# Attention and gated feed-forward on one core: a new order of evictions, statistics and turnings in the first six rows of the QKV stage

## The chip, the cores and the metric

The kernel runs on one core of a Trainium2 chip. The metric is the device time of one execution in microseconds, less being better. The engines are named as the profile names them: PE is TensorE's matmul stream and PEld its weight loads, DVE is VectorE, ACT is ScalarE, POOL is GpSimd, SP is SyncE, whose queue (SPq) issues nearly all DMAs here.

## What is computed

One layer norm feeds two branches whose results are added to the input: a sliding dilated attention (32 heads of 18, eight keys each at distances 0, 2, ... 14) with its output projection, and a gated feed-forward of width 4608. x is 2048 x 576 in bf16.

```python
def _A_ref(x, wqkv, wo):
    B, S, D = x.shape
    H = 32; Dh = D // H
    W, dil = 8, 2
    qkv = (lambda x, *d: x.transpose(*d))((x @ wqkv).reshape(B, S, 3, H, Dh), 2, 0, 3, 1, 4)
...
    logits = jnp.einsum("bhsd,bhswd->bhsw", q, kg) * scale
    logits = jnp.where(mask[None, None, :, :], logits, -1e9)
    attn = _softmax(logits, axis=-1)
    o = jnp.einsum("bhsw,bhswd->bhsd", attn, vg)
    return (lambda x, *d: x.transpose(*d))(o, 0, 2, 1, 3).reshape(B, S, D) @ wo

def _B_ref(x, w_gate, w_up, w_down):
    g = _silu(x @ w_gate)
    u = x @ w_up
    return (g * u) @ w_down

x = A_x
xn = _layernorm(x, axis=-1)
return x + _A_ref(xn, A_wqkv, A_wo) + _B_ref(xn, B_w_gate, B_w_up, B_w_down)
```

## The kernel before

The 2048 tokens are cut into 16 rows of 128. Token p*16+r lies on partition p of row r, so a row is one [128, 576] tile. The program has two stages.

**The QKV stage** goes through the rows 0 to 15. Row r needs its x, normalized and turned (channels on partitions), as xnT. A row is normalized in this order: two `bn_stats` over its halves (`ln_half`, VectorE, line 214), a `bn_aggr` that makes mean and variance of them (line 216), a square root on ScalarE (`ln_sqrt`, line 226), and `normalize`: a reciprocal (line 231), the subtraction and multiplication over 576 columns (`ln_apply`, line 237) and a copy of 64 columns that pads the row (line 243), all on VectorE. Rows 1 to 4 are turned on TensorE against an identity; for rows 2, 3 and 4 this is `transp_halves` (line 280), ten small matmuls into two PSUM tiles, of which ScalarE copies one and VectorE the other to xnT (line 284). Row 0 and the rows from 5 on are turned by a DMA on SP's queue (`transp_dma`, line 288), issued when the row is normalized. (Row 0's DMA turning is for the feed-forward; its QKV product uses a turning on TensorE and weights its sums by 1/std in the eviction.)

`p_row` issues the 36 matmuls of a row: 18 pairs, each on the two halves of TensorE's rows at once, into four PSUM tiles t[0] to t[3] of 432 columns. The first ten pairs are one half of the sums, the last eight the other half. Between the last eight, at the place `at`, `p_row` calls `between`, and there the next row's turning is issued: `at=(0, 3)` is behind four of the eight pairs, the default `(0, 1)` behind two of them. `p_evac` copies the four PSUM tiles out in six parts: part 0 is t[0] (Q), parts 1 and 2 are t[2] (K and V), parts 3 and 4 are t[1] (Q and K), part 5 is t[3] (V). The parts listed in `dve` go to VectorE (line 366, in row 0 line 368), the others to ScalarE (line 366, in row 0 line 370).

The order of all instructions on each engine is the order of the Python calls, written out by hand: the file switches the scheduler off. So an instruction that waits holds up all that stands behind it on its engine. Each DMA that SP issues takes the next of eight completion semaphores in turn, and its issue waits until the DMA eight places before it has landed.

**The feed-forward stage** goes over four token tiles (tt) of 512 tokens and nine chunks (ch) of 512 columns of the gate and up projections: `g_pair` (line 602) issues 36 pairs of matmuls for a chunk from the slot of `gu` that holds its weights, `load_gu` fills the other slot. Chunk `it` = tt*9+ch is computed while the weights of `it`+1 land; those of `it`+2 are loaded when `it` is done. The down projection (`d_half`, line 631) follows for each token tile. Its weights `wd` come in nine chunks by `load_wd` (line 193). The tile `wd` also holds the loaded and the normalized rows of x in the QKV stage, which is why chunks 0 to 6 come during the first token tile; chunk 7 (columns 16128 to 18431 of the flattened tile) and chunk 8 lie past those rows, which end at column 14335. In the first token tile SP issues, behind chunk `it`=0: the weights of `it`=2, two pieces of `wo`, three stores of V to DRAM and `load_wd(7)`; behind `it`=1: the weights of `it`=3, `load_wd(0)` and three pieces of `wo`. The attention runs on VectorE between the feed-forward's products (`chain`).

Of the kernel before, what the change touches and what calls it, by code (L numbers as in the profile page):

```python
# [70 lines left out]
def kernel(  # L71
# [11 lines left out]
    nc = tc.nc  # L83
# [95 lines left out]
    def load_gu(it):  # L179
        ch, slot = it % NCH, it % NSLOT  # L180
        fc = slice(ch * FC * P, (ch + 1) * FC * P)
        nc.sync.dma_start(gu[:, slot, 0:4, :], B_w_gate[0:512, fc].rearrange("(kt kp) n -> kp kt n", kp=P))  # L182
        nc.sync.dma_start(gu[:, slot, 4:8, :], B_w_up[0:512, fc].rearrange("(kt kp) n -> kp kt n", kp=P))
        nc.sync.dma_start(gu[0:64, slot, 8, :], B_w_gate[512:576, fc])
        nc.sync.dma_start(gu[64:128, slot, 8, :], B_w_up[512:576, fc])
# [6 lines left out]
    def load_wd(ch):  # L192
        nc.sync.dma_start(wd[:, ch * FC:(ch + 1) * FC, :],
                          B_w_down[ch * FC * P:(ch + 1) * FC * P, :].rearrange("(f p) j -> p f j", p=P))

    def new_ps(name):
        return ps.tile([P, 512], f32, name=name, tag="ps")


    ln = {}  # L200
# [6 lines left out]
    sums = {}  # L207

    def ln_half(r, k):
        c, j = divmod(r, 4)  # L210
        xc, xn, mv, rstd = ln[c]
        if k == 0:
            sums[r] = lns.tile([P, 2, 6], f32, name="stats")
        nc.vector.bn_stats(sums[r][:, k, :], xc[:, j, k * HALF:(k + 1) * HALF])  # L214
        if k == 1:
            nc.vector.bn_aggr(mv[:, j, :], sums[r][:].rearrange("p c s -> p (c s)"))  # L216

    def ln_stats(r, n=1):
        for i in range(r, r + n):
            ln_half(i, 0)  # L220
            ln_half(i, 1)

    def ln_sqrt(r, n=1):
        c, j = divmod(r, 4)
        xc, xn, mv, rstd = ln[c]
        nc.scalar.activation(rstd[:, j:j + n], mv[:, j:j + n, 1], ACT.Sqrt, bias=eps_t[:], scale=1.0)  # L226

    def ln_recip(r, n=1):
        c, j = divmod(r, 4)
        rstd = ln[c][3]  # L230
        nc.vector.reciprocal(rstd[:, j:j + n], rstd[:, j:j + n])
# [54 lines left out]
    def transp_dma(r):  # L286
        c, j = divmod(r, 4)
        nc.sync.dma_start_transpose(xnT[:, :, r * P:(r + 1) * P], ln[c][1][:, j, :] if r else xn0)
# [7 lines left out]
    def p_mm(t, g, kt, half, r, start, stop):  # L296
        rows = slice(0, P) if half is None else slice(64 * half, 64 * half + 64)
        return nc.tensor.matmul(t[g][:, 0:G], xT_of(r)[rows, kt, :], w_at(g, kt, rows),  # L298
                                start=start, stop=stop)

    def p_row0_k(t, kt, gs=range(NG)):
        for g in gs:
            p_mm(t, g, kt, None, 0, kt == 0, False)
# [6 lines left out]
    def fence_after(mm):  # L310
        f = nc.gpsimd.engine_nop()
        tc.add_manual_dep(f.ins, mm.ins.name, SYNC, reason="first half done")
        return f

    def fence_before(mm, f):
        tc.add_manual_dep(mm.ins, f.ins.name, SYNC, reason="banks change row tiles")

    def p_row(r, between=None, at=(0, 1), early=(), then=None):


        t = [None] * NG
        fence = {}

        def pair(swap, i, kt):
            for half in range(2):
                g = i + 2 * (half ^ swap)
                if t[g] is None:
                    t[g] = new_ps("qkv_ps")
                mm = p_mm(t, g, kt, half, r, swap == 0 and kt == 0, swap == 1 and kt == 3)
                if swap == 0 and kt == 3 and half == 1:  # L330
                    fence[i] = fence_after(mm)
                if swap and kt == 0 and half == 0:
                    fence_before(mm, fence[i])

        for i, kt in early:
            pair(0, i, kt)
        if then is not None:
            then()
        for swap in range(2):
            for i in range(2):  # L340
                for kt in (0, 1, 2, 3) if swap else (0, 4, 1, 2, 3):
                    if swap or (i, kt) not in early:
                        pair(swap, i, kt)
                    if swap and (i, kt) == at and between is not None:
                        between()
        return t

    def p_evac(r, t, only=range(6), between=None, last=6, dve=(5,)):


        c, j = divmod(r, 4)
        ks, vs = stage[2 * c % 4], stage[(2 * c + 1) % 4]
        vdst = vs[:, j, :].rearrange("p (d h) -> p d h", h=H)
        parts = [
            (QO[:, r, 0:G], t[0][:, 0:G]),
            (ks[:, j, HALF:D], t[2][:, 0:HALF]),
            (vdst[:, :, 0:8], t[2][:, HALF:G].rearrange("p (h d) -> p d h", d=DH)),
            (QO[:, r, G:D], t[1][:, 0:D - G]),
            (ks[:, j, 0:HALF], t[1][:, D - G:G]),
            (vdst[:, :, 8:H], t[3][:, 0:G].rearrange("p (h d) -> p d h", d=DH)),  # L360
        ]
        for n in only:
            if n == last:
                between()
            if r:
                (nc.vector.tensor_copy if n in dve else nc.scalar.copy)(*parts[n])  # L366
            elif n in dve:
                nc.vector.tensor_scalar(*parts[n], ln[0][3][:, 0:1], None, op0=ALU.mult)
            else:
                nc.scalar.mul(*parts[n], ln[0][3][:, 0:1])  # L370
# [24 lines left out]
    dve = Filler()  # L395
# [74 lines left out]
    def normalize(r, n=1):  # L470
        ln_recip(r, n)
        for i in range(r, r + n):
            ln_apply(i)
            if i > 4:
                transp_dma(i)

    def turn(r):
        return lambda: transp_halves(r)
# [21 lines left out]
    t = [new_ps("qkv_ps") for g in range(NG)]  # L500
# [14 lines left out]
    def finish_row0():  # L515
        p_row0_k(t, 3)
        p_row0_rest(t)
        p_evac(0, t, (5, 0, 3, 1, 4, 2), dve=(5, 1, 2))
        ln_half(3, 0)
        load_gu(0)  # L520
        transp_dma(0)

    u = p_row(1, turn(2), (0, 3), ((0, 0), (0, 1), (0, 2), (1, 0)), finish_row0)
    p_evac(1, u, (0, 1, 2, 3, 4), dve=(1, 2))
    ln_half(3, 1)
    ln_open(1)
    ln_half(4, 0)
    ln_sqrt(3)
    p_evac(1, u, (5,), dve=())
    normalize(3)  # L530
    for ring in (Kr, Vr):
        nc.sync.dma_start(ring[0:1, 0:HALO, :], wz[0:1, :].unsqueeze(1).to_broadcast([1, HALO, D]))

    t = p_row(2, turn(3), (0, 3))
    ln_half(4, 1)
    ln_sqrt(4)
    normalize(4)
    ln_stats(5)
    p_evac(2, t, dve=())
    ln_sqrt(5)  # L540
    normalize(5)

    t = p_row(3, turn(4))
    ln_stats(6)
# [9 lines left out]
    for r in range(4, R):  # L554
        t = p_row(r)
# [92 lines left out]
    for tt in range(NTT):  # L648
        for ch in range(NCH):
            it = tt * NCH + ch  # L650
            for p in range(2):
                g_pair(tt, ch, p)
                for j in (2 * p, 2 * p + 1):
                    g_evac(ch, j)
                    if it % NCH < NCH - 1 or p == 0:
                        dve.pump(1.4)
            if ch == NCH - 1:
                dve.drain(lambda: chains[0] > tt)
                for r in range(RT * tt, RT * tt + RT):
                    nc.sync.dma_start_transpose(oT[:, :, r * P:(r + 1) * P], QOP[:, r, :])  # L660
            if it + NSLOT < NTT * NCH:
                load_gu(it + NSLOT)
            if tt == 0:
                if 1 <= ch <= 7:
                    load_wd(ch - 1)
                if ch == 5:
                    load_wd(8)
                for _ in range(3 if ch in (1, 2) else 2):
                    if wo_order:
                        load_wo(wo_order.pop(0))  # L670
                if ch == 0:
                    store(2, 3, 3)
                    load_wd(7)
            if ch == 7:
                for i in (0, 2):
                    nc.sync.dma_start(xr[:, i:i + 2, :], x_v[:, RT * tt + i:RT * tt + i + 2, :])
            if ch == 1 and tt < NTT - 1:
                chain(tt + 1)
        for sub in range(0, RT, 2):
            t, fence = {}, {}  # L680
            for swap in range(2):
                for i in (sub, sub + 1):
                    d_half(tt, i, swap, t, fence)
                    if swap:
                        dve.pump(12.5 if i == sub else 4.0)
                        d_out(RT * tt + i, i, t[i])
# [30 lines left out]
```

## Time and profile before

| | |
|---|---|
| median of 3 runs | 505.66 us (504.88 to 505.94) |
| profiled execution, own time | 505.31 us |
| its span (first to last instruction) | 503.5 us |
| mean granted TensorE clock | 1.00 |
| QKV stage, first feed-forward matmul at | 60.98 us |

The profile is of one execution. A timeline row gives the start and the length in microseconds, engine, line, operation, what is written and read, and how many instructions are merged into the row; in brackets stands how long the engine was idle before it and who ended that. Lengths of neighbouring instructions on DVE and ACT overlap by some hundredths of a microsecond, so the next one may start a little before the last one ends. The chain of waits gives, in order of time, the pieces of the path that ended last.

### The profile page before, as it was taken

Reading aid. Unit: us, or ns where it says so; the run is one execution under the profiler, and the core shown is the slowest. Engines: PE = TensorE matmul, PEld = TensorE weight load, DVE = VectorE, ACT = ScalarE, POOL = GpSimd, SP = SyncE. Lnnn points to the kernel's source line nnn. Section 1 sums busy time; section 2 is a strip of 40 time slices with the busy share of each in tenths; the row PEclk is TensorE's granted clock in tenths of the full one; section 3 lists DMA queues with packets and bytes.
Section 4 is the critical chain, followed back from the end, with each engine's and each line's share of the span. In section 5 each row is a group of like instructions: output and inputs, shape, how many; then the busy total and the mean of one; then the engine's idle time right before and its main releaser. Section 6 shows DMA issues by size and latency. Waiting matters only on the chain.

```text
span 503.5 us, 13277 instructions
## 1 busy us (share of the span) xinstructions
PE 498.8 (99%) x5799; PEld 375.5 (75%) x5799; DVE 329.7 (65%) x480; ACT 200.2 (40%) x415; POOL 2.6 (1%) x9
## 2 busy tenths in 40 slices
PE   9999999999999999999999999999999999999997
PEld 4566654444788888888888888888888888888886
DVE  5788499898998698999898129995990222221001
ACT  4666656655400164555300354558000454553000
POOL 2000000000000000000000000000000000000000
PEclk9999999999999999999999999999999999999999
DMA  8699999879931036446731054455600335452100
GB/s 320 159 196 239 287 295 292 255 246 303 241 107 61 25 107 223 158 127 211 156 98 39 26 187 125 159 183 154 143 25 14 99 108 184 140 191 38 28 14 25
DMA packets 77186, 75.42 MB, mean 150 GB/s; under 512 B 22708, under 2 KB 72528, under 8 KB 77128
## 3 DMA queue, kind: packets, MB, share of 16 engines
q1 hardware_dynamic: 76840, 73.98, 49.8%
q8 instruction: 45, 0.74, 0.6%
q10 hardware_dynamic: 288, 0.59, 0.4%
q14 instruction: 13, 0.11, 0.1%
HBM read 58.76 MB, written 5.90 MB: 128 GB/s over the span
## 4 chain that ended last, share of the span: by engine, by line
PE 97%; DMA 2%; DVE 1%; ACT 0%; issue 0%; SPq 0%
PE g_ps L602 54%; PE d_ps L631 32%; PE qkv_ps L298 10%; DMA gu<-in_B_w_up_dram 2%; PE warm_ps L174 1%; DVE stats L214 0%; PE pt L259 0%; ACT QO L366 0%; ACT rstd L226 0%; DVE xnT L284 0%; ACT hT L366 0%; DVE wd L237 0%; DVE mv L216 0%; ACT ot L645 0%; SPq L182 0%
## 5 line engine op out<-in xcount | busy, mean ns | idle before, releaser
L602 PE MATMUL g_ps<-xnT,gu 64*128 64x512 bf16 x2592 | 281.4, 376 | 0.2 <-DMA gu<-in_B_w_up_dram 0.2
L602 PEld LDWEIGHTS <-gu 64*128 64x128 bf16 x2592 | 206.3, 94 | 73.9 <-DMA gu<-in_B_w_up_dram 0.7
L631 PE MATMUL d_ps<-wd,hT 64*128 64x288 bf16 x2304 | 150.5, 283 | 0.0
L613 ACT ACTIVATE sg<-g_ps 128x512 bf16<-128x512 f32 x144 | 87.4, 607 | 157.1 <-PE g_ps L602 157.1
L631 PEld LDWEIGHTS <-hT 64*128 64x128 bf16 x2304 | 122.6, 94 | 21.7
L615 DVE TENSOR_TENSOR hT<-sg,uc 128x512 bf16<-128x512 bf16 x144 | 60.1, 419 | 94.2 <-ACT uc L614 94.0
L614 ACT CAST uc<-g_ps 128x512 bf16<-128x512 f32 x144 | 85.5, 594 | 0.0
L417 DVE TENSOR_REDUCE PP<-PP 128x64 f32<-128x1152 bf16 x64 | 84.9, 1346 | 0.4
L298 PE MATMUL qkv_ps<-hT,xnT 64*128 64x432 bf16 x540 | 50.5, 343 | 0.8 <-ACT QO L366 0.8
L412 DVE TENSOR_TENSOR PP<-QO,Kr 128x2304 bf16<-128x2304 bf16 (+1 forms) x35 | 43.5, 1250 | 7.6 <-DMA Kr<-hT 7.4
L643 DVE TENSOR_TENSOR ot<-d_ps,xr 128x288 bf16<-128x288 f32 x30 | 12.3, 451 | 51.0 <-PE d_ps L631 51.0
L298 PEld LDWEIGHTS <-xnT 64*128 64x128 bf16 x540 | 29.7, 94 | 20.0 <-ACT QO L366 1.2
L444 DVE TENSOR_TENSOR PP<-Vr,A 128x2304 bf16<-128x2304 bf16 (+1 forms) x35 | 43.3, 1251 | 0.4
L449 DVE TENSOR_TENSOR PP<-PP 128x2304 bf16<-128x2304 bf16 x24 | 32.5, 1354 | 0.3
L631 PE MATMUL d_ps<-wo,xnT 64*128 64x288 bf16 x288 | 27.0, 283 | 0.0
L613 ACT ACT_TABLE_LOAD x5 | 6.4, 1283 | 47.5 <-PE g_ps L602 47.5
L366 ACT CAST hT<-qkv_ps 128x288 bf16<-128x288 f32 (+2 forms) x58 | 21.2, 426 | 0.1
L631 PEld LDWEIGHTS <-xnT 64*128 64x128 bf16 x288 | 17.5, 94 | 2.8
L437 ACT ACTIVATE PP<-PP 128x1024 f32<-128x1024 f32 x4 | 4.2, 1056 | 31.2 <-DVE PP L433 31.2
L645 ACT CAST ot<-d_ps 128x288 bf16<-128x288 f32 x1 | 0.4, 398 | 38.7 <-PE d_ps L631 38.7
L366 ACT CAST QO<-qkv_ps 128x432 bf16<-128x432 f32 (+1 forms) x30 | 12.2, 409 | 8.0 <-PE qkv_ps L298 8.0
L214 DVE BATCH_NORM_STATS2 stats<-wd 128x6 f32<-128x288 bf16 x32 | 12.9, 441 | 2.4 <-DMA wd<-in_A_x_dram 2.4
(53 smaller groups left out, 91.7 us busy)
## 6 DMA issues: line engine op xcount, KB each, us to landing
gu<-in_B_w_gate_dram SPq DMA_DIRECT2D x36, 512.0 KB, 3.8
gu<-in_B_w_up_dram SPq DMA_DIRECT2D x36, 512.0 KB, 5.1
wd<-in_B_w_down_dram SPq DMA_DIRECT2D x9, 576.0 KB, 6.0
kv_d<-hT SPq DMA_DIRECT2D x5, 576.0 KB, 6.1
gu<-in_B_w_gate_dram SPq DMA_DIRECT2D x36, 64.0 KB, 4.8
gu<-in_B_w_up_dram SPq DMA_DIRECT2D x36, 64.0 KB, 4.4
xr<-in_A_x_dram SPq DMA_DIRECT2D x8, 288.0 KB, 4.6
out_dram<-ot SPq DMA_DIRECT2D x16, 144.0 KB, 1.8
```

The costliest lines, as they stand in the source:

```text
L214: nc.vector.bn_stats(sums[r][:, k, :], xc[:, j, k * HALF:(k + 1) * HALF])
L298: return nc.tensor.matmul(t[g][:, 0:G], xT_of(r)[rows, kt, :], w_at(g, kt, rows), start=start, stop=stop)
L366: (nc.vector.tensor_copy if n in dve else nc.scalar.copy)(*parts[n])
L412: nc.vector.tensor_tensor(prod[:, a:b], QO[:, RT * tt + a:RT * tt + b, :], Kr[:, s:s + b - a, :], op=ALU.mult)
L417: nc.vector.tensor_reduce(L[:, w, rs], prod[:, rs].rearrange("p r (h d) -> p r h d", d=DH), axis=AX.X, op=ALU.add)
L444: nc.vector.tensor_tensor(dst[:, a:b], Vr[:, s:s + b - a, :].rearrange("p r (d h) -> p r d h", h=H), A[:, w, a:b].unsqueeze(2).to_broadcas ...
L449: nc.vector.tensor_tensor(dst, acc, pv, op=ALU.add)
L602: mm = nc.tensor.matmul(ring_ps[j][b][:], gu[rows, slot, k, fc], xnT[rows, kt, tok], start=(swap == 0 and kt == 0), stop=(swap == 1 and kt ...
L613: nc.scalar.activation(sg[:], t[0][:], ACT.Silu)
L614: nc.scalar.copy(uc[:], t[1][:])
L615: nc.vector.tensor_tensor(hT[:, ch * FC + j, :], sg[:], uc[:], op=ALU.mult)
L631: mm = nc.tensor.matmul(t[sub][h][:, 0:HALF], a[rows], w[rows, h * HALF:(h + 1) * HALF], start=(swap == 0 and n == 0), stop=(swap == 1 and ...
```

## The change

In rows 0 to 5 the order of VectorE's and ScalarE's instructions is new. Row 0's part 1 goes from VectorE to ScalarE, behind part 4; both halves of row 3's statistics come before row 2's turning is copied, and their `bn_aggr` behind it, ahead of row 1's evictions; row 2's turning is issued one pair of matmuls earlier and row 3's two pairs earlier; the root of row 3 comes between parts 0 and 3 of row 1's evictions on ScalarE; row 4's statistics come behind row 3's normalization, row 5's ahead of row 2's evictions; rows 4 and 5 share one root and one reciprocal. And `load_wd(7)` is issued behind row 1, ahead of row 5's turning on SP's queue, no longer behind chunk 0 of the feed-forward.

```diff
@@ -212,13 +212,16 @@
         if k == 0:
             sums[r] = lns.tile([P, 2, 6], f32, name="stats")
         nc.vector.bn_stats(sums[r][:, k, :], xc[:, j, k * HALF:(k + 1) * HALF])
-        if k == 1:
-            nc.vector.bn_aggr(mv[:, j, :], sums[r][:].rearrange("p c s -> p (c s)"))
+
+    def ln_aggr(r):
+        c, j = divmod(r, 4)
+        nc.vector.bn_aggr(ln[c][2][:, j, :], sums[r][:].rearrange("p c s -> p (c s)"))
 
     def ln_stats(r, n=1):
         for i in range(r, r + n):
             ln_half(i, 0)
             ln_half(i, 1)
+            ln_aggr(i)
@@ -515,30 +518,30 @@
     def finish_row0():
         p_row0_k(t, 3)
         p_row0_rest(t)
-        p_evac(0, t, (5, 0, 3, 1, 4, 2), dve=(5, 1, 2))
+        p_evac(0, t, (5, 0, 3, 2, 4, 1), dve=(5, 2))
         ln_half(3, 0)
+        ln_half(3, 1)
         load_gu(0)
         transp_dma(0)
 
-    u = p_row(1, turn(2), (0, 3), ((0, 0), (0, 1), (0, 2), (1, 0)), finish_row0)
-    p_evac(1, u, (0, 1, 2, 3, 4), dve=(1, 2))
-    ln_half(3, 1)
+    u = p_row(1, turn(2), (0, 2), ((0, 0), (0, 1), (0, 2), (1, 0)), finish_row0)
+    ln_aggr(3)
+    p_evac(1, u, (0, 1, 2), dve=(1, 2))
+    ln_sqrt(3)
+    p_evac(1, u, (3, 4, 5), dve=())
+    normalize(3)
     ln_open(1)
-    ln_half(4, 0)
-    ln_sqrt(3)
-    p_evac(1, u, (5,), dve=())
-    normalize(3)
+    ln_stats(4)
     for ring in (Kr, Vr):
         nc.sync.dma_start(ring[0:1, 0:HALO, :], wz[0:1, :].unsqueeze(1).to_broadcast([1, HALO, D]))
-
-    t = p_row(2, turn(3), (0, 3))
-    ln_half(4, 1)
-    ln_sqrt(4)
-    normalize(4)
+    load_wd(7)
+
+    t = p_row(2, turn(3))
     ln_stats(5)
-    p_evac(2, t, dve=())
-    ln_sqrt(5)
-    normalize(5)
+    p_evac(2, t, (0, 1, 2), dve=())
+    ln_sqrt(4, 2)
+    p_evac(2, t, (3, 4, 5), dve=())
+    normalize(4, 2)
@@ -670,7 +673,6 @@
                 if ch == 0:
                     store(2, 3, 3)
-                    load_wd(7)
```

## The prediction

> **What bounds the kernel now.** I read the page's chain of waits first, then the same chain in order of time, then the timeline of PE and of VectorE around the places where the chain leaves PE.
>
> ```profile
> PE 97%; DMA 2%; DVE 1%; ACT 0%; issue 0%; SPq 0%
> ```
>
> ```profile
> 16.35 0.49 DVE xnT L284
> ...
> 21.38 39.60 PE qkv_ps L298 x432
> ...
> 76.97 7.62 DMA gu<-in_B_w_up_dram
> ...
> 84.64 46.94 PE g_ps L602 x431
> 131.59 39.66 PE d_ps L631 x646
> 171.24 70.04 PE g_ps L602 x648
> ```
>
> PE sets the time but for two places: from row 3's copy at 16.35 to 21.38 the path runs over VectorE and ScalarE, and before 84.64 over the landing of the up weights of chunk 3. Only time that PE loses there can be won. How much it is:
>
> ```profile
> 12.41 0.31 PE L280 MATMUL pt<-ident,wd 64*128 64x64 bf16 x10
> 12.55 3.60 PE L298 MATMUL qkv_ps<-hT,xnT 64*128 64x432 bf16 x36
> 15.98 0.33 PE L280 MATMUL pt<-ident,wd 64*128 64x64 bf16 x10
> 16.12 3.24 PE L298 MATMUL qkv_ps<-hT,xnT 64*128 64x432 bf16 x32
> 19.18 0.33 PE L280 MATMUL pt<-ident,wd 64*128 64x64 bf16 x10
> 19.32 1.28 PE L298 MATMUL qkv_ps<-hT,xnT 64*128 64x432 bf16 x12
> ```
>
> From row 4 on 432 matmuls take 39.60 us without a break, 0.183 for a pair, 3.30 for a row's 36. The 36 between the turnings of rows 2 and 3 take 15.98 - 12.55 = 3.43, so 0.13 is lost; the next 32 take 19.18 - 16.12 = 3.06 in place of 2.93, another 0.13. The last 12 should end at 19.32 + 1.10 = 20.42, and row 4 begins at 21.38: 0.96 lost. That makes **1.22 us in the QKV stage**. In the feed-forward the first token tile lasts from 21.38 + 39.60 = 60.98 to 131.59, 70.61 us, the second 70.04: **0.57 us** more, and the chain has one place in it that is not PE, the weights before 84.64.
>
> The three losses in the QKV stage have one form. Each row waits for the second half of its turning, which VectorE copies:
>
> ```profile
> 10.82 1.37 DVE L368 TENSOR_SCALAR hT<-qkv_ps,rstd 128x432 bf16<-128x432 f32 x3 [0.25 <-PE qkv_ps L298]
> 12.10 0.45 DVE L214 BATCH_NORM_STATS2 stats<-wd 128x6 f32<-128x288 bf16 x1
> 12.79 0.49 DVE L284 CAST xnT<-pt 128x320 bf16<-128x320 f32 x1 [0.23 <-PE pt L280]
> 13.19 0.66 DVE L366 CAST hT<-qkv_ps 128x288 bf16<-128x288 f32 x2
> ...
> 18.57 0.81 DVE L214 BATCH_NORM_STATS2 stats<-wd 128x6 f32<-128x288 bf16 x2
> 19.42 0.21 DVE L216 BATCH_NORM_AGGREGATE mv<-stats 128x2 f32<-128x12 f32 x1
> 19.99 0.16 DVE L231 RECIPROCAL rstd<-rstd 128x1 f32<-128x1 f32 x1 [0.36 <-ACT rstd L226]
> 20.19 0.43 DVE L237 TENSOR_SCALAR wd<-wd,mv,rstd 128x576 bf16<-128x576 bf16 x1
> 20.66 0.18 DVE L243 COPY wd<-wd 128x64 bf16<-128x64 bf16 x1
> 20.75 0.48 DVE L284 CAST xnT<-pt 128x320 bf16<-128x320 f32 x1
> ```
>
> Row 4's copy ends at 21.23 and PE starts at 21.38, 0.15 later; I use 0.15 for every row. (The chain goes over a QO eviction that ends at nearly the same time; the copy fits rows 2 and 3 as well.) PE had turned row 4 at 19.18, but the copy stands on VectorE behind row 5's normalization, which waits for row 5's root on ScalarE (the bracket at 19.99).
>
> **The change part by part.** I follow the new order with these lengths. A VectorE copy of a turning starts 0.38 behind PE's turning (12.79 - 12.41), and the next instruction 0.40 behind its start (13.19 - 12.79). ScalarE:
>
> ```profile
> 12.75 0.42 ACT L284 CAST xnT<-pt 128x320 bf16<-128x320 f32 x1 [0.87 <-PE pt L280]
> 13.07 0.71 ACT L366 CAST QO<-qkv_ps 128x432 bf16<-128x432 f32 x2
> ```
>
> *Row 0's part 1 goes to ScalarE.*
>
> ```profile
> L368 DVE TENSOR_SCALAR hT<-qkv_ps,rstd 128x288 bf16<-128x288 f32 x1 | 0.5, 508 | 0.0
> ```
>
> The instruction itself takes 0.51, 0.43 without its overlap. VectorE is done with row 0 at 12.19 - 0.43 = 11.76 and starts row 3's statistics near 11.68; both halves take 0.81 and end at 12.49. On ScalarE part 1 now waits for VectorE's part 2, as both read t[2]; a wait that was not there. It starts near 11.80 and takes some 0.5 (0.508 above). Behind it stands the copy of row 2's turning, due at 12.23 + 0.34 = 12.57, so the wait has 0.27 of cover; without that cover row 2 would start later by what is missing.
>
> *Row 2's turning one pair earlier*: 12.41 - 0.18 = 12.23. VectorE's copy runs from 12.61 to 13.10, so PE may start row 2 at 13.25. PE wants it after the turning (0.14) and five pairs (0.92), at 13.29. The first 0.13 is gone, by a hair: 0.04.
>
> *Row 3.* `bn_aggr` at 13.01 ends at 13.22; a reciprocal can follow 0.36 later (19.42 + 0.21 to 19.99), root included, so at 13.58 and, as ScalarE's copy at 12.57 and part 0 at 12.89 stand ahead of the root, near 13.65. VectorE meanwhile evicts parts 1 and 2 until 13.72 (13.14 and 0.66, less an overlap of 0.08), then reciprocal, normalization from 13.92, pad until 14.57. The turning stands two pairs earlier, behind 12 pairs (2.20) of a row that starts at 13.29: 15.49. It has 0.9 to spare. Row 4's statistics run from 14.48 to 15.53, ahead of the copy, which starts at 15.87 and ends at 16.36; PE may start row 3 at 16.51 and wants it at 15.49 + 0.14 + 1.10 = 16.73. The second 0.13 is gone, with 0.22 to spare.
>
> *Rows 4 and 5 together.* Row 5's statistics follow the copy, 16.27 to 17.33 (0.81, 0.04, 0.21). The joint reciprocal follows 0.36 later, at 17.69, since ScalarE is through parts 0 to 2 of row 2 by then (their 576 + 144 columns from 16.2 on, some 0.9 by the 0.71 of two such parts above); row 4's normalization begins 0.20 later, at 17.89, and its pad ends at 18.54; row 5's take from 18.45 to 19.10. PE turns row 4 behind 12 pairs of row 3: 16.73 + 2.20 = 18.93, 0.4 after its pad. VectorE is free at 19.01, so the copy goes from 19.31 to 19.79, PE may start row 4 at 19.94 and wants it at 18.93 + 1.24 = 20.17. So PE meets no wait, and **row 4 starts at 20.17 in place of 21.38: 1.21 us won**. From there VectorE is 1.44 ahead of its old times (20.75 to 19.31) and PE 1.21, so rows 5 to 15, which had no wait, get none. The bounds of this part: 1.22 is all that was lost; if each of the some ten links between 15.87 and 19.31 were 0.1 longer than in the rows, row 4 would start 0.7 late and 0.5 would be won.
>
> *The load of chunk 7.* It is 576 KB on a queue that is in use:
>
> ```profile
> 5.00:18.00 13.00, 12.98 (x136) 7.03 (x136) 9.82 (x32) 6.43 (x20) 1.73 (x3) 1.00 1.05 356
> 18.00:22.00 4.00, 3.22 (x46) 1.85 (x43) 3.45 (x12) 3.25 (x12) 0.00 (x0) 1.00 0.01 3
> 60.00:69.00 9.00, 9.00 (x89) 4.75 (x84) 8.90 (x8) 6.33 (x14) 0.00 (x0) 1.00 0.98 313
> 69.00:76.50 7.50, 7.50 (x72) 3.96 (x70) 7.50 (x10) 3.84 (x8) 0.00 (x0) 1.00 0.81 262
> 76.50:92.40 15.90, 15.74 (x144) 7.45 (x141) 12.29 (x22) 11.43 (x19) 0.00 (x0) 1.00 1.01 304
> ```
>
> The last two columns are the DMA engines' busy share and GB/s. In the old place the chunk (0.59 MB) goes out just ahead of chunk 3's weights into a full stretch: at 304 GB/s it holds what is behind it for 1.9 us. Those weights are 0.57 late. Whether the queue keeps its order or the transfers share it, 0.59 MB less has to pass before they have landed; a third of the 1.9 is enough. So **0.57 won**; if the next chunk becomes the late one, part of it comes back, so the bounds are 0 and 0.57. In the new place it stands behind two small issues, of which this is the last:
>
> ```profile
> 13.93 0.82 SPq L532 DMA_DIRECT2D Vr<-ot  x1
> ```
>
> So it is issued near 14.8, when the weights of chunk 0 still fill the queue, and needs 0.59 MB / 356 GB/s = 1.7 us behind them, in a stretch that was idle (0.01). Row 5's DMA turning stands behind it:
>
> ```profile
> xnT<-A SPq DMA_TRANSPOSE x1, 7.0
> ...
> xnT<-wd SPq DMA_TRANSPOSE x1, 2.6
> ```
>
> These are row 0's, behind a full queue, and row 5's. Row 5's is now issued at 19.13 (its pad's end); with 2.6 it lands at 21.7, with the whole 1.7 on top at 23.4, and PE wants row 5 at 20.17 + 3.30 = 23.47. No loss. The Trainium skill ("DMA: Bandwidth & Descriptors", section "Queues, rings and completion order") says that each DMA engine takes up the descriptors of a ring in order; by that rule row 5's turning would pay for whatever of chunk 7 is still queued, which speaks against this move. Chunk 0's weights were through by 18, so by the rule chunk 7 is through by 19.7 and the sum stays; row 0's turning, which took 7.0 behind chunk 0's weights, agrees with it.
>
> **Sum.** The profiled execution took 505.31 us, its span 503.5 and 1.8 around it. 505.31 - 1.21 - 0.57 = 503.53. It stands 0.35 below the median shown, 505.66, from which the same sum gives 503.88. I say 503.7.
>
> **The rivals.**
>
> *The weights stay late.* Chunk 4's weights are issued when chunk 3's have landed, in the same full stretch; freed of one stall PE asks for them 0.57 earlier. For it: the busy share of 1.01 until 92.40. Against: less is in the queue. Then only 1.21 is won: 504.1 to 504.4, say 504.3.
>
> *VectorE's chain still ends last.* The rows' lengths hold, but each link is 0.1 slower in the new neighbourhood: row 4 starts near 20.9, 0.5 + 0.57 won, 504.4. For it: margins of 0.04 and 0.2; against: the same pairs of instructions stood together before.
>
> *The transfers set the pace.* At 60 to 69 us the DMAs are full (0.98), and if they, and not PE, decide when chunk 2's weights land, the gain of the first rows turns into a wait in the feed-forward; only 0.57 or less stays: 505.1 to 505.6. Against: the stream begins with row 5's turning, which is issued 1.7 earlier, and from 69.00 to 76.50 the share is 0.81, so chunk 2's weights do not land at the last moment.
>
> *Slower: row 5's turning is late behind chunk 7.* If it takes the 7.0 us of row 0's, it lands at 26.1, PE waits 2.6 at row 5, and 1.21 + 0.57 - 2.6 makes it 0.85 slower: 506.3. It costs from a landing time of 4.3 us on (23.47 - 19.13), and the change is slower from 6.1.
>
> **How the numbers follow.** Forecast 0.52, the weights stay late 0.16, VectorE's chain 0.12, the transfers 0.11, row 5's turning 0.09. Differences under 0.2% (1.0 us) can't be told from none. The forecast and the first two lie at 0.25 to 0.39% faster, of which I count 0.08 as lost to the spread of the runs (1.06 us between three): faster 0.72. The third and that 0.08 make 0.19 for no change, and slower has 0.09. The range is 502.8 (all won at the lowest run, 504.88 - 1.78 = 503.1, and 0.3 for a spread like that between the profiled execution and the median) to 505.3, which takes in the first two rivals with the spread of the runs and part of the third; the forecast alone has 503.1 to 504.4.
>
> **What would show it.** Right: row 4's first matmul at 20.1 to 20.4 and no wait of PE on line 284's copies; row 3's copy on VectorE near 15.9 and row 4's near 19.3; row 5's DMA turning issued near 19.1 and landed within 4 us; the first feed-forward matmul near 59.8; no wait on the weights of chunk 3, the first token tile at 70.0 to 70.1. Wrong: a wait of PE at row 5 or 6 for a DMA, VectorE's copy of row 4 after 19.6, or a stall at chunk 3 or 4 of the feed-forward.

## The result and the profile after

The changed kernel takes 503.63 us, the median of 12 runs (503.29 to 505.02); the kernel before, beside it on the same chip, 505.12 us (12 runs, 504.60 to 506.45). The ratio is 0.9971, with a 95% interval of 0.9961 to 0.9980: faster by 0.3%. The profiled execution took 503.73 us, with a span of 501.9, 1.58 less than the one before.

The chain of waits on the page of the changed kernel, in shares of the span, and below it rows of the same chain in order of time (start, length, what):

```profile
PE 99%; DVE 0%; issue 0%
```

```profile
12.70 0.15 PE pt L283 x10
...
19.53 40.51 PE qkv_ps L301 x444
60.04 69.93 PE g_ps L605 x648
129.97 39.69 PE d_ps L634 x648
169.66 69.93 PE g_ps L605 x648
```

The chain is PE from end to end; the 2% of DMA and 1% of VectorE are gone from it. The first token tile of the feed-forward, gate, up and down together, now takes 169.66 - 60.04 = 109.62 us, and the second tile's gate and up part has the same 69.93 as the first: no stall on weights. In the chain before it was 171.24 - 60.98 = 110.26. So 0.64 of the 1.58 us came out of that tile. The other 0.94 was there before it began (60.98 to 60.04).

PE's timeline of the changed kernel around the turnings of rows 2, 3 and 4 (the code has moved down by three lines, so the turning is line 283 and its copies 287):

```profile
12.54 0.31 PE L283 MATMUL pt<-ident,wd 64*128 64x64 bf16 x10
12.68 3.27 PE L301 MATMUL qkv_ps<-hT,xnT 64*128 64x432 bf16 x34
15.79 0.31 PE L283 MATMUL pt<-ident,wd 64*128 64x64 bf16 x10
15.93 3.45 PE L301 MATMUL qkv_ps<-hT,xnT 64*128 64x432 bf16 x36
19.22 0.31 PE L283 MATMUL pt<-ident,wd 64*128 64x64 bf16 x10
19.36 7.83 PE L301 MATMUL qkv_ps<-hT,xnT 64*128 64x432 bf16 x84
```

At 0.183 for a pair, 34 matmuls should take 3.11 and 36 should take 3.29. From 12.68 to 15.79 are 3.11, from 15.93 to 19.22 are 3.29: nothing is lost at rows 2 and 3. The last group begins with the 12 matmuls that are left of row 3, so row 4 begins at 19.36 + 1.10 = 20.46, without a break.

VectorE's timeline says why. In the brackets stand the idle time before an instruction and what ended it:

```profile
12.92 0.49 DVE L287 CAST xnT<-pt 128x320 bf16<-128x320 f32 x1
...
16.16 0.49 DVE L287 CAST xnT<-pt 128x320 bf16<-128x320 f32 x1 [0.39 <-PE pt L283]
...
17.98 0.17 DVE L234 RECIPROCAL rstd<-rstd 128x2 f32<-128x2 f32 x1 [0.36 <-ACT rstd L229]
...
19.59 0.49 DVE L287 CAST xnT<-pt 128x320 bf16<-128x320 f32 x1 [0.21 <-PE pt L283]
```

Before, PE waited for VectorE's copy. Now VectorE stands idle for 0.39 and 0.21 until PE has turned the row. The wait for the root is still in VectorE's row (0.36 at 17.98) and still ahead of row 4's copy, but it comes earlier: rows 4 and 5 are both normalized before PE has turned row 4.

The DMA side: SP's timeline, and from the view of DMA issues the median time from issue to landing, for the stretches around 15.0 and 19.4 us:

```profile
15.03 0.52 SPq L193 DMA_DIRECT2D wd<-in_B_w_down_dram  x1
19.41 6.83 SPq L291 DMA_TRANSPOSE xnT<-wd  x3
```

```profile
wd<-in_B_w_down_dram SPq DMA_DIRECT2D x1, 576.0 KB, 6.6
...
xnT<-wd SPq DMA_TRANSPOSE x1, 2.8
```

Chunk 7 landed at 21.6, row 5's turning at 19.41 + 2.8 = 22.2, and PE wanted row 5 at 20.46 + 3.30 = 23.76. Two stretches of the changed kernel by time (the last two columns are the DMA engines' busy share and GB/s):

```profile
18.00:22.00 4.00, 4.00 (x56) 2.21 (x54) 3.25 (x11) 3.28 (x11) 0.00 (x0) 1.00 0.91 186
...
76.50:92.40 15.90, 15.90 (x150) 7.20 (x148) 12.50 (x21) 12.13 (x20) 0.00 (x0) 1.00 0.88 276
```

The load filled a stretch that had been empty (0.01), and the stretch around chunk 3's weights went from a share of 1.01 to 0.88, with PE busy all through.

### The profile page after: what moved, and what is told of

The parts are those of the page before. It is cut to its first block, busy times and chain, and to the rows that moved or that the text cites. A ratio compares the mean times of both kernels' runs of the same rounds, so it can differ in the third digit from the quotient of the medians.

```text
span 501.9 us, 13275 instructions
## 1 busy us (share of the span) xinstructions
PE 498.0 (99%) x5799; PEld 283.0 (56%) x5799; DVE 329.0 (66%) x478; ACT 200.5 (40%) x415; POOL 2.6 (1%) x9
## 4 chain that ended last, share of the span: by engine, by line
PE 99%; DVE 0%; issue 0%
PE g_ps L605 56%; PE d_ps L634 32%; PE qkv_ps L301 11%; PE warm_ps L174 1%; PE pt L262 0%; DVE ot L648 0%; PE pt L283 0%; PE warm_ps L262 0%; PE warm_ps L177 0%
## 5 line engine op out<-in xcount | busy, mean ns | idle before, releaser
L605 PEld LDWEIGHTS <-gu 64*128 64x128 bf16 x2592 | 126.1, 94 | 152.9
L634 PE MATMUL d_ps<-wd,hT 64*128 64x288 bf16 x2304 | 146.4, 283 | 0.0
L634 PEld LDWEIGHTS <-hT 64*128 64x128 bf16 x2304 | 112.0, 94 | 29.8
L301 PEld LDWEIGHTS <-xnT 64*128 64x128 bf16 x540 | 26.0, 94 | 22.4 <-ACT xnT L287 0.2
L634 PE MATMUL d_ps<-wo,xnT 64*128 64x288 bf16 x288 | 22.9, 283 | 0.0
L634 PEld LDWEIGHTS <-xnT 64*128 64x128 bf16 x288 | 14.0, 94 | 3.6
```

Of the source, the lines that this page charges most:

```text
L605: mm = nc.tensor.matmul(ring_ps[j][b][:], gu[rows, slot, k, fc], xnT[rows, kt, tok], start=(swap == 0 and kt == 0), stop=(swap == 1 and kt ...
L634: mm = nc.tensor.matmul(t[sub][h][:, 0:HALF], a[rows], w[rows, h * HALF:(h + 1) * HALF], start=(swap == 0 and n == 0), stop=(swap == 1 and ...
```

## The experiments

Eleven kernels ran beside the kernel before, each in five rounds. Times are medians with the lowest and highest run; "QKV" is the time from the turning of row 2 to the first feed-forward matmul by the chain of waits, which leaves out differences of the start (47.34 us in the changed kernel: 60.04 - 12.70). In the kernels with the old places of the turnings row 2's comes one pair, 0.18, later, so that 0.18 is to be added to their value (load alone, turnings) and to that of the kernel before, 60.98 - 12.57 = 48.41.

| kernel | us | ratio to before, 95% interval | QKV |
|---|---|---|---|
| changed, once more | 503.69 (503.53 to 504.89) | 0.9969 [0.9957, 0.9981] | 47.34 |
| new order, old place of the load | 503.90 (503.35 to 505.39) | 0.9973 [0.9964, 0.9982] | 47.34 |
| old order, new place of the load | 504.82 (504.50 to 505.76) | 0.9989 [0.9978, 1.0000] | 48.40 |
| two roots | 504.24 (503.48 to 507.57) | 0.9988 [0.9970, 1.0006] | 51.51 |
| two roots, old place of the load | 503.69 (503.41 to 505.12) | 0.9977 [0.9967, 0.9987] | 47.34 |
| row 4's statistics late | 503.87 (503.79 to 504.08) | 0.9970 [0.9958, 0.9982] | 47.83 |
| old places of the turnings | 503.75 (503.60 to 507.58) | 0.9975 [0.9959, 0.9992] | 47.45 |
| load behind row 7 | 504.47 (503.70 to 505.49) | 0.9985 [0.9972, 0.9998] | 48.26 |
| load 2 us sooner | 503.55 (503.37 to 504.67) | 0.9970 [0.9960, 0.9980] | 47.34 |
| two chunks | 505.21 (503.72 to 509.35) | 1.0011 [0.9991, 1.0030] | 47.34 |
| four loads | 513.73 (511.57 to 514.26) | 1.0148 [1.0122, 1.0174] | 58.10 |

The kernels ran in three sets, each beside the kernel before, whose medians were 505.26 (new order alone, load alone, two roots, row 4's statistics), 505.19 (changed kernel once more, turnings, behind row 7, four loads) and 504.91 (the other three). Between sets the ratios can be compared better than the times.

In two of the expectations below (the changed kernel once more, and the load 2 us sooner) "row 4's first matmul" means the first matmul behind row 4's turning; row 4's own comes 1.10 later.

### The new order alone

```diff
-    load_wd(7)
...
                     store(2, 3, 3)
+                    load_wd(7)
```

> The new order of rows 0 to 5 alone; chunk 7 is loaded at its old place, behind chunk 0 of the feed-forward. My theory (the two parts win separately, 1.21 and about 0.6 us): row 4 starts about 1.2 us earlier after row 1's first matmul than in the kernel before, the first feed-forward matmul comes 1.2 us earlier, the stall on the weights of chunk 3 stays (0.5 to 0.7 us), and the time is 1.0 to 1.3 us under the kernel before, a ratio of 0.9974 to 0.9980. Rival (the transfers set the pace): the stall at chunk 3 grows by about what the first rows win, and the time is within 0.3 us of the kernel before.

The QKV stage is that of the changed kernel, to the hundredth. In the profiled execution (505.25 us) PE stalled in the feed-forward. Its chain:

```profile
59.99 23.33 PE g_ps L604 x216
...
83.77 8.59 DMA gu<-in_B_w_up_dram
...
92.41 39.13 PE g_ps L604 x359
131.54 39.66 PE d_ps L633 x646
```

Gate and up of the first tile take 131.54 - 59.99 = 71.55 in place of 69.93, and it is chunk 4's weights that are awaited, not chunk 3's. That execution is one of the two slowest of twelve. The lowest run, 503.35, is like that of the changed kernel (503.29), so in the best executions the load's place makes no difference. The new order gives 505.26 - 503.90 = 1.36 us between the medians, and by the table 48.41 + 0.18 - 47.34 = 1.25 in the QKV stage.

### The load alone

The old order of rows 0 to 5, with `load_wd(7)` behind row 1.

> The old order of rows 0 to 5 with chunk 7 loaded behind row 1. My theory: row 4 starts where it did (21.4 us, give or take 0.3 of the start), no stall at chunk 3 or 4, the first token tile of the feed-forward takes 0.55 to 0.7 us less, a ratio of 0.9986 to 0.9990. Rival (the stall moves to chunk 4): less than 0.2 us won.

PE's timeline and the chain of this kernel:

```profile
19.54 1.28 PE L298 MATMUL qkv_ps<-hT,xnT 64*128 64x432 bf16 x12
21.59 2.73 PE L298 MATMUL qkv_ps<-hT,xnT 64*128 64x432 bf16 x28 [0.78 <-ACT QO L366]
```

```profile
61.19 69.93 PE g_ps L604 x648
```

Row 4 could begin at 19.54 + 1.10 = 20.64 and begins at 21.59, so 0.95 is lost as before; the first tile has no stall. Medians: 505.26 - 504.82 = 0.44 won, with an interval that reaches 1.0000; lowest runs: 504.48 and 504.50, nothing won.

### One root for rows 4 and 5, or two

```diff
     ln_stats(4)
+    ln_sqrt(4)
...
     t = p_row(2, turn(3))
+    normalize(4)
     ln_stats(5)
...
-    ln_sqrt(4, 2)
+    ln_sqrt(5)
...
-    normalize(4, 2)
+    normalize(5)
```

> The changed kernel, but rows 4 and 5 have a root and a reciprocal each: row 4's root stands on ScalarE ahead of row 3's turning, its normalization on VectorE ahead of row 5's statistics. My theory: what frees row 4 is that its statistics run in VectorE's idle time ahead of row 3's copy, not the joint root, so no wait of PE comes back and the time is that of the changed kernel within 0.2 us. Rival (the joint root saves a wait of 0.36 and a reciprocal of 0.2 on the path): row 4 starts 0.3 to 0.5 us later, and the time is 0.3 to 0.5 us above the changed kernel.

The median is higher, but not for want of the joint root: the five lowest runs, 503.48 to 503.58, are like those of the changed kernel (503.29 to 503.51, once more 503.53 to 503.67), and PE has no wait at row 4. But three of twelve runs lie above 506. One of them is the profiled one (507.51 us). Its chain, PE's waits, and two stretches behind the wait (the third column from the right is the granted clock):

```profile
19.18 6.61 DMA xnT<-wd
...
25.83 37.95 PE qkv_ps L301 x396
```

```profile
PE qkv_ps L301 <- DMA xnT<-wd: 2.4, 1, 2.4
```

```profile
25.90:29.00 3.10, 3.10 (x18) 1.26 (x20) 2.48 (x10) 0.29 (x1) 0.00 (x0) 0.50 0.87 253
29.10:32.00 2.90, 2.90 (x34) 1.53 (x32) 0.98 (x4) 1.73 (x6) 0.00 (x0) 0.98 1.01 197
```

Row 5's turning took 6.6 us to land where it takes 2.8 in the changed kernel. PE waited 2.4, and then ran for 3.1 us with a granted clock of 0.50: 18 matmuls in place of 34, another 16 x 0.0915 = 1.5. Together that is 3.9 of the 51.51 - 47.34 = 4.17 lost. This is the wait of the prediction's slower rival, in a neighbour of the changed kernel. Its reason, the bytes of chunk 7, is not shown by this profile: the chunk, issued at 15.17, took 7.8 and landed at 23.0, and the turning landed 2.8 later.

### Two roots without the load ahead of row 5

> The kernel with two roots, with chunk 7 put back to its old place in the feed-forward part. Theory (the late turnings of row 5 come from chunk 7's bytes ahead of them): row 5's turning lands within 4 us in the profile, no run lies above 505.5, and what spread is left is the wait for chunk 3's or 4's weights (lowest 503.4 to 503.6, median 503.9 to 504.3). Rival (they come from something that the load has nothing to do with): two or more of about twelve runs lie above 506 again, as with the early load (three of twelve).

No run of twelve lies above 505.12, where the same order with the load ahead had three above 506. That fits the load as the cause, but three against none in twelve runs does not show it: the changed kernel has the load ahead too, and none of its 23 runs lies above 505.02. The profiled execution, with the load in its old place, has no stall in the feed-forward either; a row of its chain, and its stretch from 18 to 22:

```profile
59.82 69.93 PE g_ps L606 x648
```

```profile
18.00:22.00 4.00, 4.00 (x56) 2.19 (x52) 3.09 (x12) 3.69 (x12) 0.00 (x0) 1.00 0.32 57
```

Without the load this stretch moves 57 GB/s, with it 186. The difference over 4 us is 0.52 MB, so most of chunk 7's 0.59 MB went out after 18 us.

### Row 4's statistics behind row 3's copy

```diff
     ln_open(1)
-    ln_stats(4)
...
     t = p_row(2, turn(3))
-    ln_stats(5)
+    ln_stats(4, 2)
```

> The changed kernel, but row 4's statistics stand behind row 3's copy on VectorE, next to row 5's; the joint root stays. My theory: two statistics halves and an aggregation (0.81 + 0.13 to 0.25 us) go onto the path from row 3's copy to row 4's, which has 0.22 to 0.25 to spare; VectorE's copy of row 4 starts about 0.7 to 0.8 later than in the changed kernel, PE waits 0.4 to 0.8 us at row 4, and the time is 0.4 to 0.8 above the changed kernel. Rival (the joint root is what matters): no wait, the time of the changed kernel within 0.2 us.

The chain from row 4's root on:

```profile
18.32 0.30 ACT rstd L229
...
19.34 0.42 PE pt L283 x10
19.76 40.52 PE qkv_ps L301 x444
```

With row 4's statistics behind row 3's copy, 1.0 us more on VectorE, the chain leaves PE again. It costs 47.83 - 47.34 = 0.49 in the profile, and 503.79 - 503.35 = 0.44 between the lowest runs of this kernel and of the new order alone, beside it; between the medians it does not show (ratios of 0.9970, and 0.9971 for the changed kernel). The wait is no longer at the copy but at the turning, whose input is normalized too late. So the new order has room for about 0.5 us more on VectorE ahead of row 4.

### The old places of the turnings

```diff
-    u = p_row(1, turn(2), (0, 2), ((0, 0), (0, 1), (0, 2), (1, 0)), finish_row0)
+    u = p_row(1, turn(2), (0, 3), ((0, 0), (0, 1), (0, 2), (1, 0)), finish_row0)
...
-    t = p_row(2, turn(3))
+    t = p_row(2, turn(3), (0, 3))
```

> The changed kernel with the turnings of rows 2 and 3 put back to their old place in the matmuls of the row before. Theory (the two waits of 0.13 on VectorE's copy of the turning were won by the earlier turning, not by the shorter chain of VectorE): PE waits 0.1 to 0.2 for VectorE's copy before row 2 and again before row 3, row 4's first matmul 0.2 to 0.4 later than in the changed kernel, times up by 0.2 to 0.4 (lowest run 503.5 to 503.7). Rival (the copies were late because VectorE was busy): VectorE is free in the new order, the copies start at once, and the place makes no difference: lowest run 503.3, no gap of PE at the copies.

PE's timeline:

```profile
12.52 3.60 PE L301 MATMUL qkv_ps<-hT,xnT 64*128 64x432 bf16 x36
15.94 0.33 PE L283 MATMUL pt<-ident,wd 64*128 64x64 bf16 x10
16.08 3.24 PE L301 MATMUL qkv_ps<-hT,xnT 64*128 64x432 bf16 x32
19.14 0.33 PE L283 MATMUL pt<-ident,wd 64*128 64x64 bf16 x10
```

36 matmuls take 15.94 - 12.52 = 3.42, 0.13 too much; 32 take 3.06, 0.13 too much. These are the two losses of the kernel before, back with the places, though VectorE stands idle ahead of these copies here. (By the table 47.45 + 0.18 - 47.34 = 0.29 is lost.) In the times the 0.2 to 0.4 expected do not show: the medians are 503.75 and, for the changed kernel beside it, 503.69, the lowest runs 503.60 and 503.53. One run of twelve, 507.58, lies far above the rest.

### The load behind row 7

```diff
-    load_wd(7)
...
     normalize(7)
+    load_wd(7)
```

> The new order of rows 0 to 5 is kept, but chunk 7 of the down projection weights is issued on SP's queue behind row 7's DMA turning (near 25 us) instead of behind row 1 (15.0 us). Theory: the load only has to leave the stretch around chunk 3's weights of the feed-forward part, and any place in the QKV part does that; out of the way of row 5's turning it takes away the executions in which that turning takes 6 to 7 us. So: first token tile of the feed-forward part 70.0 to 70.1, as in the changed kernel, row 5's turning at 2.5 to 4.0 us to landing, lowest run 503.3, median 503.4 to 503.7, no run above 505.5. Rival (the late turnings have nothing to do with chunk 7): the spread of the runs stays as in the changed kernel and in the kernel with two roots. Rival (place matters for the feed-forward part): the first token tile goes back above 70.5 and the median to 504.0.

A miss. The first tile had its 69.93 and row 5's turning landed in 2.9 us, but the median is 0.8 above the changed kernel's. SP's timeline, PE's timeline, and the waits of PE's weight loads:

```profile
25.61 0.58 SPq L193 DMA_DIRECT2D wd<-in_B_w_down_dram  x1
...
28.64 3.53 SPq L291 DMA_TRANSPOSE xnT<-wd  x2
```

```profile
25.76 7.83 PE L301 MATMUL qkv_ps<-hT,xnT 64*128 64x432 bf16 x84
34.34 4.00 PE L301 MATMUL qkv_ps<-hT,xnT 64*128 64x432 bf16 x41 [0.75 <-ACT rstd L229]
```

```profile
PEld L301 <- DMA xnT<-wd: 1.2, 1, 1.2
```

PE stops ahead of row 8. The timeline puts it down to a root on ScalarE, but the weight loads of PE, which go first, waited for a DMA turning. Row 8's turning, issued at 28.64 behind the load and three writes of K, landed at 34.3, 5.7 later. In the changed kernel it is issued at 28.54 and lands at 32.4, once more at 27.84 and 31.5, 3.9 and 3.6 later. So the load's place is not free: here row 8's turning is late behind it, where row 5's was not late enough to matter behind row 1.

### More bytes ahead of row 5's turning

Two chunks, 7 and 8, behind row 1:

> The changed kernel with chunk 8 of the down projection weights behind chunk 7, so that twice the bytes stand ahead of row 5's turning, both issued before the turning is ready. Theory (ring order): 576 KB more at the 186 GB/s that the stretch from 18 to 22 us moved are 3.2 us, so row 5's turning lands near 25.4 instead of 22.2, PE waits some 2.3 us before row 5 and runs slower for some us behind it: 506 to 508. Rival (the time went into issuing the three loads, which kept SP until 23.5, and not into the rings): SP is free at 16.5 here, the turning lands by 23.5, and the time is that of the changed kernel, 503.4 to 504.0.

Four loads behind row 1 (the two chunks, the residual rows of the first token tile and chunk 1 of the gate and up weights):

> The changed kernel with three more transfers behind row 1, next to chunk 7: chunk 8 of the down projection weights, the first token tile of the residual input and chunk 1 of the gate and up weights, all in front of row 5's DMA turning on SP's queue. Theory (the turning's descriptors stand behind the bytes queued ahead of them on each engine's ring): about four times the bytes ahead put the landing of row 5's turning at 25 to 28 us instead of 22.2, PE waits 2 to 4 us before row 5, and with the lower clock after such a wait the time is 506 to 509. Rival (the turning takes its share beside the loads): it lands by 23.5, PE waits for nothing before row 5, and the time is 503.4 to 504.0.

With two chunks the profiled execution was the fastest of the twelve, 503.72. From its view of DMA issues, and its stretch from 18 to 22:

```profile
xnT<-wd SPq DMA_TRANSPOSE x1, 4.3
```

```profile
18.00:22.00 4.00, 4.00 (x56) 2.21 (x54) 3.23 (x11) 3.28 (x11) 0.00 (x0) 1.00 1.08 282
```

The turning landed at 19.44 + 4.3 = 23.7. PE needed it at 23.79 and did not stop, though its weight loads had waited 0.2 for it. The median, 505.21, lies under the 506 to 508 expected. Nine of twelve executions were above 505, three of them above 507, which fits the expected wait in most of them; no profile of one of these was taken. With four loads the wait is in the profile, and the lowest of five runs is 511.57. SP's timeline there, a row of the chain, and PE's wait:

```profile
22.76 0.59 SPq L185 DMA_DIRECT2D gu<-in_B_w_up_dram  x1
23.46 7.11 SPq L291 DMA_TRANSPOSE xnT<-wd  x3
```

```profile
23.46 9.16 DMA xnT<-wd
```

```profile
PE qkv_ps L301 <- DMA xnT<-wd: 9.1, 1, 9.1
```

This is worse than expected, since two things add up: SP was still issuing the loads when the turning was ready, which made it some 4 us late, and from 23.46 it took another 9.2 us to land, behind the bytes. The rival, that the turning takes its share beside the loads, falls.

### The load 2 us sooner, and the changed kernel once more

```diff
     u = p_row(1, turn(2), (0, 2), ((0, 0), (0, 1), (0, 2), (1, 0)), finish_row0)
+    load_wd(7)
     ln_aggr(3)
...
-    load_wd(7)
```

> The changed kernel with chunk 7 issued some 2 us sooner on SP's queue: ahead of the two writes of zeros into the rings, at about 12.7 us instead of 14.9. Theory (what decides is how soon chunk 7's bytes are through before row 5's turning): the chunk lands before 21 instead of at 21.4 to 21.6, row 5's turning at 21.8 to 22.2, lowest run 503.3 to 503.5, median 503.4 to 503.7, none above 504.9. Rival (the rings of the engines are full until 18 anyway, so that the order of issue before that changes nothing): chunk 7 lands at 21.4 to 21.7 as before, and the times are those of the changed kernel. It would cost time only if the input rows of later rows came later by it: row 4's first matmul would then start after 19.6.

> The changed kernel once more, unaltered, on the chip of the other three, as their measure: lowest run 503.3, median 503.6, row 4's first matmul 19.2 to 19.6 and its first token tile of the feed-forward part at 69.9 to 70.1. If row 5's turning is late in some executions of it too, as in the kernel with two roots, one run in ten or more lies above 504.8.

The chunk issued at 12.85 took this long to land:

```profile
wd<-in_B_w_down_dram SPq DMA_DIRECT2D x1, 576.0 KB, 9.0
```

It landed at 21.9, not sooner than when issued at 14.90 to 15.03 (21.4 to 21.6), so the theory falls. The rival's reason is not shown either: the engines moved 334 GB/s from 17.6 to 19.5 and 9 from there to 20.3, so most of the bytes went sooner than in the changed kernel (291 GB/s until 20.4, with a start 0.3 later), and only the landing came no sooner. The times, ratios of 0.9970 and 0.9969, can't be told apart. The changed kernel once more had row 4's first matmul at 20.22 (19.12 as the expectation counts, just ahead of its 19.2 to 19.6) and its first tile at 69.93. Of its 23 runs in both sets two, 504.89 and 505.02, lie above the 504.8 that the expectation took as a mark of late turnings. Neither is as late as the 3.9 us that the wait cost with two roots, so the late turning of its neighbours has not shown itself in it. No version tried beats it by more than the spread.

## Why the prediction was right

**The order.** The prediction had 1.21 us won in the QKV stage, with row 4 at 20.17, counted from a turning of row 2 at 12.23: 7.94 between them. It measured 20.46 - 12.54 = 7.92. The profiled execution began 0.31 later, at the ten matmuls of row 0, ahead of everything that was changed; once more, row 4 began at 20.22. The new order alone gave 1.36 between the medians. All three losses went where the steps said: the two of 0.13 by the earlier turnings (they come back with the old places), the 0.96 by row 4's statistics in VectorE's idle time ahead of row 3's copy, so that row 5's root and normalization are done before row 4 is turned (half of it comes back with the statistics late). The margins were real but small. Row 2's, 0.04 in the prediction, held; row 4's is about 0.5 us of VectorE time. Part 1 of row 0 on ScalarE cost nothing: the copy of row 2's turning started when PE had turned it. Its move, and that of row 3's statistics, were not tried alone.

**The joint root** was followed as a step, but wins nothing by itself: two roots give the same lowest runs.

**The load.** This term was right for the profiled execution (0.57 forecast, 0.64 measured), but sized on the wrong ground. It took the stall of one profiled execution as a property of the kernel. The runs show a stall that comes and goes: with the load in its old place one profile of the new order had 1.6 us of it, another (with two roots) none. Between the medians the load's place is worth 0.44 in the old order. In the new one the ratios are 0.9973 with the old place and 0.9971 with the new, 0.1 us, which can't be told from nothing; with two roots the load ahead costs, 0.9988 against 0.9977 or 0.55 us, with intervals that overlap. In the lowest runs it is worth nothing.

**The number** was in part luck. The forecast of 503.7 started from one execution (505.31) and the median of three (505.66); from the median of twelve, 505.12, the same sum gives 505.12 - 1.78 = 503.34. That the load's term was too large for the new order made up for the start. The gain between the medians, 505.12 - 503.63 = 1.49, lies between the 1.21 of the order alone and the forecast sum of 1.78. That the old order's median carries some of the stalls fits its 0.44, but is not shown.

**Row 5's turning.** "No loss" held for the changed kernel: issued at 19.41 (19.13 forecast, with the 0.31 of the start), landed 2.8 us later. But a step ahead of it failed: that chunk 7 is through by 19.7, "0.59 MB / 356 GB/s = 1.7 us" behind chunk 0's weights. It landed at 21.4 to 21.6. Row 0's turning (128 x 640 in bf16, 0.16 MB), which SP issues between the two, was left out, and the rate was not steady:

```profile
18.40:18.90 0.50, 0.50 (x10) 0.24 (x7) 0.47 (x3) 0.44 (x2) 0.00 (x0) 1.00 0.65 28
18.90:20.40 1.50, 1.50 (x28) 0.88 (x26) 1.25 (x5) 0.84 (x3) 0.00 (x0) 1.00 1.00 291
```

For half a microsecond the engines moved 28 GB/s, then 291, and the landing came 1.2 after that. Why they paused stays open.

So the slower rival had more room than its 0.09, but its reason held only in part. In three profiles row 5's turning landed 0.5 to 0.7 behind the chunk ahead of it: with row 4's statistics late (chunk 23.0, turning 23.5), with the load 2 us sooner (21.9 and 22.5) and with two chunks (23.1 and 23.7). With four loads it landed behind them. With two roots chunk 7 landed no later than in the first of these, at 23.0, and the turning at 25.8; from 22.9 to then the engines moved 60 GB/s. So the wait that PE had there did not come from chunk 7's bytes alone. The rival's price was also too low, as its 506.3 counted the wait of 2.6 but not the slower clock behind it; two roots, with a wait of 2.4, took 507.51.

**The other rivals.** The weights stayed late only with the load in its old place, and there at chunk 4 as that rival had it. VectorE's chain ended last only when 1.0 us were put on it. The transfers did not set the pace: QKV's gain of 1.2 us reached the end.

**What stays open.** Why row 5's turning took 6.6 us in one profile and 2.8 in others of nearly the same kernel; the last 2.8 came after chunk 7 had landed. Runs of 507 come now and then in other kernels too (the kernel before has one of 507.93 among 29), so a single high run does not say that a turning was late; only the profiled one does.

## What to carry to other kernels

On an engine that works in order, look for an instruction that PE waits for behind one that itself waits for another engine: put what can run early (here the statistics) into the engine's idle time, and the copy where its input arrives, and the chain falls back to PE. A prefetch into an empty stretch of the DMA queue can be paid by the next transfer that PE needs on the same queue: count its bytes, and how late that transfer may land, before choosing the place; here one chunk behind row 1 cost nothing in the changed kernel's runs, behind row 7 it cost 0.8 us between the medians, and two behind row 1 were too many. A stall in one profiled execution is a sample: compare the lowest runs and the medians with the edit alone before giving it a price.

## What the runs showed of the hardware

A pause of PE of 2.4 us was enough to halve the granted clock: 0.50 over the next 3.1 us, then 0.98 again, in the kernel with two roots. After a pause of 0.75, with the load behind row 7, it stayed at 1.00 (34 matmuls in the next 3.1 us). After 9.1 us, with four loads, it was 0.51 for as long as after 2.4:

```profile
32.70:35.80 3.10, 3.10 (x18) 1.32 (x20) 0.00 (x0) 0.00 (x0) 0.00 (x0) 0.51 1.15 276
```

So a wait of 2.4 or 9.1 costs its own length and about 1.5 us more. The Trainium skill ("TensorE: Matmul & The Clock Gate", section "HAM oscillation — how this bites in real kernels") gives the rule that idle gaps of PE should stay below some 3.4 us. The trace differs: the gap of 2.4 us was shorter, and the clock fell all the same; the measurement decides.

Row 5's turning by what was queued ahead of it, from issue to landing: 2.6 to 2.9 us with nothing, 2.6 to 3.4 with one chunk (6.6 in one profile), 4.3 with two chunks, 9.2 with four loads. And after the change the next room is small. The waits of the changed kernel have one of its weight loads for a DMA turning:

```profile
PEld L301 <- DMA xnT<-wd: 0.2, 1, 0.2
```

It is row 6's, and PE itself did not stop. By this profile a still earlier row 4 would meet that turning; it was not tried.
